# Taking chunk 0 of a gated MLP's second half column-first over two token tiles, and one more bank skipped before the spatial products

## The chip, the cores and the metric

The kernel runs on one core of a Trainium2 chip. The metric is the device time of one execution in microseconds (us). Three runs of the kernel as it stood gave 703.43, 703.61 and 705.5, median 703.61. One further execution was profiled: it took 703.75 us, and its profile covers a span of 702.0 us. Times inside the kernel are given in us from the start of that span.

## The reference

One transformer block on 2048 tokens of width 1024, in bfloat16, with two residual parts:

```python
h  = x + A(layernorm(x))      # qkv, attention over 8 earlier tokens at distance 0,2,..,14, then @ wo
h2 = h + B(layernorm(h))
# B:
z  = gelu(x @ w_in)                       # (2048, 3584)
z1 = z[..., :1792]
z2 = layernorm(z[..., 1792:])
g  = w_sp @ z2 + b_sp[:, None]            # (2048, 2048) times (2048, 1792)
return (z1 * g) @ w_out
```

The part that matters here is `z2`: the last 1792 columns of `x @ w_in`, through GELU, then normalised along those 1792 columns, so that a token's mean and variance need all 1792 of them. The product with `w_sp` (the spatial products) needs `z2` of all tokens.

## The kernel before

The tokens are cut into 4 chunks of 512 (`NCH`), a chunk into 4 token tiles of 128 (`TPC`, index `il`). The work of a chunk c is: layer norm and transposition; `qkv(c, ..)` (line 461); `attention(c)`, almost all of it on the vector engine (DVE): products of q with shifted k (line 525), sums of them by halving (lines 529, 532, 535), a small sum over heads on the tensor engine (PE, line 555), softmax, a small spreading matmul (line 617), products with v (lines 638, 641, 649); `head(c)`: the product with `wo` (line 716, 4 tiles of 16 matmuls), the residual on DVE (line 722), its squares on the scalar engine (ACT, line 727), the second layer norm (lines 678 to 687 and 759) and a transposition by DMA into `hnT`; `b_z2(c)` (line 790) and `b_z1(c)` (line 856). After all chunks come the spatial products in a form with seven products of halves instead of eight (`times`, line 1066), and the output product (line 1164).

`b_z2(c)` works token tile by token tile. A tile has 1792 columns, in two parts given by `win_specs`: `hf` 0 has 1024 columns and the weights `win0`, `hf` 1 has 768 columns and the weights `win1`. A part is summed over eight steps of 128 rows (`kt`), each step two matmuls (512 and 512 columns, or 512 and 256), 16 matmuls in all. Below, z2(il, hf) is one such part. Its GELU on ACT (line 797) frees the PSUM space, and when both parts of a tile are there, ACT sums the squares (line 805). When the four tiles of chunk 0 are done, DVE forms the variance (line 811 and lines 678 to 681), GpSimd (POOL) raises it to the power -1/2 (lines 685 and 687), and ACT normalises (line 831).

The order of work on PE, ACT, DVE and POOL is worked out before the program is written: `Order` holds a list of operations with an assumed duration, dependencies, priority and slots, plays them through in assumed time, and emits each engine's instructions in the order of the assumed starts. On the chip every engine then works through its own list in that order, and waits at an instruction whose inputs are not there. Operations of `b_z2` and `b_z1` have priority 6 and a running number and so fill the time in which PE has nothing of `attention` or `head` to do; `head` has priority 4 and up, the attention's matmuls 1.

Three accumulators (`new_acc`, `ps_acc`, each two banks of PSUM) are shared by all of this; two more banks belong to the attention. After `o_.run()` all eight banks go to the pool `psq`, from which the spatial products take single banks; before the first of them, `bank` tiles are asked for and never written, six of them in the kernel before.

The transfers that the change and the prediction touch: the weights `win0` to `win3` come on POOL's queue (`load_win`, line 387), one after the other; `win1` is issued after the load of k for attention 2. On the queue of SyncE (SP) stand, in this order around the change, the stores of the last qkv parts (line 473), three loads of `xr` (the residual's x tiles, three buffers, line 697), then the first store of h (line 724), the load of the fourth `xr` tile into the buffer of the first, and the other stores of h. The fourth load waits until ACT has squared the first tile (line 727), because that writes into the same buffer.

Before the change the engines have, in the stretch in question:

- PE: the last qkv part, z2(0,0) with 16 matmuls, 12 matmuls of z2(0,1), the 64 of `head(1)`, the remaining 4 of z2(0,1), then z2(1,0), z2(1,1) and so on to z2(3,1), then z1 of chunk 0, with the attention's matmuls of line 555 after 40 of them.
- DVE: the end of attention 1, two products of attention 2, the residual of `head(1)`'s first tile, two sums, the residual of the second tile, and so on.
- ACT: GELU of z2(0,0), squares of three tiles of `head(1)`, GELU of z2(0,1), squares of the fourth tile, then the rest.

Of the kernel before, what the change touches and what calls it, by code (L numbers as in the profile page):

```python
# [10 lines left out]
FP32 = mybir.dt.float32  # L11
BF16 = mybir.dt.bfloat16
# [3 lines left out]
ACTF = mybir.ActivationFunctionType  # L16
# [5 lines left out]
F, FH = 3584, 1792  # L22
P = 128
NT = S // P
CH = 512
NCH = S // CH
TPC = CH // P
TPP = 2 * TPC
KT = D // P
# [39 lines left out]
class Order:  # L69
# [6 lines left out]
    def add(self, eng, us, fn, deps=(), prio=5.0, lat=0.1, take=None, free=None, table=None):  # L76
        o = _Op()
        o.eng, o.us, o.fn, o.prio, o.lat, o.free, o.table = eng, us, fn, prio, lat, free, table
        o.take = (take,) if isinstance(take, str) else take or ()
        o.deps = [d if isinstance(d, tuple) else (d, d.lat) for d in deps if d is not None]  # L80
        o.start, o.end, o.n = None, None, len(self.ops)
        self.ops.append(o)
        return o
# [49 lines left out]
def kernel(  # L133
# [13 lines left out]
    V, A, T = nc.vector, nc.scalar, nc.tensor  # L147
# [42 lines left out]
    bp = bph_stack.enter_context(tc.tile_pool(name="bph", bufs=2))  # L190
# [4 lines left out]
    def new_acc():  # L195
        return ps_acc.tile([P, 2, CH], FP32, name="acc", tag="acc")
# [7 lines left out]
    l1 = bph_stack.enter_context(tc.tile_pool(name="ln1", bufs=2))  # L204
# [167 lines left out]
    for half in range(2):  # L372
        acc = new_acc()
# [8 lines left out]
    win_specs = [(FH, 1024), (FH + 1024, 768), (0, 1024), (1024, 768)]  # L382
    wins = {}
# [11 lines left out]
    add = o_.add  # L395
    G = {}

    def dma_op(us, fn, deps, lat=0.1, free=None):
        return add("DMA", us, fn, deps, lat=lat, free=free)
# [46 lines left out]
    def order():  # L446
        seq[0] += 1
        return 6.0 + seq[0] * 1e-3
# [225 lines left out]
    def batch_rstd(key, sums, sqs, n, pfx, deps, prio, cols=TPC):  # L674
        def moments():
            t = {k: bp.tile([P, cols], FP32, name=pfx + k, tag=pfx + k) for k in ("nmean", "msq", "var", "rstd", "nb")}
            G[key] = t
            V.tensor_scalar(t["nmean"][:], sums(), -1.0 / n, None, op0=ALU.mult)
            V.tensor_tensor(t["msq"][:], t["nmean"][:], t["nmean"][:], op=ALU.mult)
            V.scalar_tensor_tensor(t["var"][:], sqs(), 1.0 / n, t["msq"][:], op0=ALU.mult, op1=ALU.subtract)  # L680
            V.tensor_scalar(t["var"][:], t["var"][:], 0.0, EPS, op0=ALU.max, op1=ALU.add)
        s1 = add("DVE", 0.74, moments, deps, prio=prio)
        def root():
            t = G[key]
            nc.gpsimd.tensor_tensor(t["rstd"][:], t["var"][:], nhalf[:, 0:cols], op=ALU.pow)
            if cols == TPC:
                nc.gpsimd.tensor_tensor(t["nb"][:], t["nmean"][:], t["rstd"][:], op=ALU.mult)
        return add("POOL", 1.05 if cols < TPC else 1.6, root, [s1], lat=0.4 if cols < TPC else 1.2)
# [79 lines left out]
    hnTs, pools = {}, {}  # L768


    def b_z2(c):
        st = {}
        sqd = []
        for il in range(TPC):
            evs = []
            for hf in range(2):
                wd = win_specs[hf][1]
                deps = [G.get(("hnT", c, il), G["hnT", c]), G["win", hf]]
                for part in range(4):
                    def mm(part=part, hf=hf, il=il, wd=wd):  # L780
                        if part == 0:
                            st["acc"] = G["accz", c, il, hf] = new_acc()
                            if il == 0 and hf == 0:
                                st["sums"] = bp.tile([P, TPC, 2], FP32, name="sums", tag="sums")
                                st["sqs"] = bp.tile([P, TPC], FP32, name="sqs", tag="sqs")
                        accf = G["accz", c, il, hf][:].rearrange("p a b -> p (a b)")
                        for kt in range(2 * part, 2 * part + 2):
                            for n0 in range(0, wd, CH):
                                n1 = min(n0 + CH, wd)
                                T.matmul(accf[:, n0:n1], hnTs[c][:, il, kt, :], wins[hf][:, kt, n0:n1],  # L790
                                         start=(kt == 0), stop=(kt == KT - 1))
                    m_ = add("PE", 0.8634 if hf == 0 else 0.650, mm, deps, prio=order(), take="acc" if part == 0 else None)
                    deps = [(m_, 0.0)]
                def ev(hf=hf, il=il, wd=wd):
                    if hf == 0:
                        st["u", il] = l1.tile([P, FH], BF16, name="u", tag="x4k", bufs=4)
                    A.activation(st["u", il][:, hf * 1024:hf * 1024 + wd], G["accz", c, il, hf][:].rearrange("p a b -> p (a b)")[:, 0:wd],
                                 ACTF.Gelu_apprx_tanh, accum_out=st["sums"][:, il, hf:hf + 1])
                evs.append(add("ACT", 1.02 if hf == 0 else 0.93, ev, [m_] + ([G["z2st", c - 1, il]] if c else []),
                               prio=2.0, free="acc", lat=0.25, table="gelu"))  # L800
            if c == 0:
                evs[0].deps += [(o, 0.1) for o in wabs_ops]
            def sq(il=il):
                junk = pools["bq"].tile([P, FH], BF16, name="junk", tag="junk", bufs=1)[:]
                A.activation(junk, st["u", il][:], ACTF.Square, accum_out=st["sqs"][:, il:il + 1])
            sqd.append(add("ACT", 1.72, sq, evs + [G["open"]], prio=5.0, lat=0.25))
        each = c == NCH - 1
        def st_tot(il=0, n=TPC):
            if il == 0:
                st["stot"] = bp.tile([P, TPC], FP32, name="stot", tag="stot")  # L810
            V.tensor_tensor(st["stot"][:, il:il + n], st["sums"][:, il:il + n, 0], st["sums"][:, il:il + n, 1], op=ALU.add)
        if not each:
            s0 = add("DVE", 0.16, st_tot, sqd, prio=2.0)
            rs = batch_rstd(("l3", c), lambda: st["stot"][:], lambda: st["sqs"][:], FH, "l3", [s0], 2.0)
        for il in range(TPC):
            i = c * TPC + il
            if each:
                s0 = add("DVE", 0.16, lambda il=il: st_tot(il, 1), [sqd[il]], prio=0.5)
                rs = batch_rstd(("l3", c, il), lambda il=il: st["stot"][:, il:il + 1], lambda il=il: st["sqs"][:, il:il + 1],
                                FH, f"l2_{il}", [s0], 0.5, cols=1)  # L820
            def nrm(il=il, i=i, part=1):
                if each:
                    t = G["l3", c, il]
                    V.tensor_scalar(st["u", il][:], st["u", il][:], t["nmean"][:], t["rstd"][:], op0=ALU.add, op1=ALU.mult)
                    dma_w(z2_d[i * P:(i + 1) * P, :], st["u", il][:])
                    return
                t = G["l3", c]
                z2 = st["u", il]
                if Z2ACT[c] > il:
                    cols = slice(part * FH // 2, (part + 1) * FH // 2)  # L830
                    A.activation(z2[:, cols], st["u", il][:, cols], ACTF.Identity, scale=t["rstd"][:, il:il + 1], bias=t["nb"][:, il:il + 1])
                else:
                    V.tensor_scalar(z2[:], st["u", il][:], t["nmean"][:, il:il + 1], t["rstd"][:, il:il + 1], op0=ALU.add, op1=ALU.mult)
                if part:
                    dma(z2_d[i * P:(i + 1) * P, :], z2[:])
            if Z2ACT[c] > il:
                n_ = add("ACT", 1.05, lambda f=nrm: f(part=0), [rs], prio=5.5)
                n_ = add("ACT", 1.05, nrm, [n_], prio=5.5)
            else:
                n_ = add("DVE", 0.75 if each else 0.62, nrm, [rs], prio=0.6 if each else 2.5)  # L840
            G["z2st", c, il] = dma_op(3.0, lambda: None, [n_])
            G["z2n", c, il] = n_
# [208 lines left out]
    p2 = ctx.enter_context(tc.tile_pool(name="p2", bufs=2))  # L1051
    psq = ctx.enter_context(tc.tile_pool(name="psq", bufs=8, space=PSUM))

    for _ in range(6):
        psq.tile([P, CH], FP32, name="bank", tag="bank", bufs=8)

    def bank():
        return psq.tile([P, CH], FP32, name="bank", tag="bank", bufs=8)
# [9 lines left out]
    def f32(name):  # L1068
        return p2.tile([P, CH], FP32, name=name, tag=name)
# [12 lines left out]
    for pr in range(NCH // 2):  # L1082
# [5 lines left out]
        for i in range(NQ):  # L1088
# [3 lines left out]
            p1, p7, p5, u = f32("p1"), f32("p7"), f32("p5"), f32("u2")  # L1092
# [60 lines left out]
        for il in range(2 * TPC):  # L1153
# [15 lines left out]
            if t < NT - 1:  # L1169
                acc = [bank(), bank()]  # L1170
# [6 lines left out]
            else:  # L1177
                for n, (lo, hi) in enumerate(LAST_COLS):
                    acc = bank()
# [53 lines left out]
```

## Time and profile before

| what | value |
|---|---|
| median of three runs | 703.61 us |
| profiled execution, its own time / its span | 703.75 / 702.0 us |
| granted PE clock in the profile | 1.00 in every stage |
| PE busy | 693.4 us, 99% of the span |
| DVE busy | 508.4 us, 72% |
| ACT busy | 276.5 us, 39% |
| POOL busy | 120.7 us, 17% |
| z2 and z1 matmuls (lines 790 and 856) | 98.2 and 98.0 us |
| spatial products (line 1066) | 448 + 336 matmuls, on PE from 432.62 |
| load of `win1` on POOL's queue | issued 185.54, 11.8 us to landing |
| fourth `xr` load on SP's queue | issued 205.44, 8.0 us to landing |

Busy time of an engine alone says little here, since DVE is the busier engine's partner in some stages and idle in others. What is to be read is which engine waits for which at a given place. In the groups and the timeline a line gives the start, the length, the engine, the source line, and in brackets the idle time of that engine just before and what ended it. In the chain a line gives start, length, and what the time was spent on; matmul ends are modelled, so starts there stand some 0.17 us later than in the timeline.

### The profile page before, as it was taken

Reading aid. Unit: us, or ns where it says so; the run is one execution under the profiler, and the core shown is the slowest. Engines: PE = TensorE matmul, PEld = TensorE weight load, DVE = VectorE, ACT = ScalarE, POOL = GpSimd, SP = SyncE. Lnnn points to the kernel's source line nnn. Section 1 sums busy time; section 2 is a strip of 40 time slices with the busy share of each in tenths; the row PEclk is TensorE's granted clock in tenths of the full one; section 3 lists DMA queues with packets and bytes.
Section 4 is the critical chain, followed back from the end, with each engine's and each line's share of the span. In section 5 each row is a group of like instructions: output and inputs, shape, how many; then the busy total and the mean of one; then the engine's idle time right before and its main releaser. Section 6 shows DMA issues by size and latency. Waiting matters only on the chain.

```text
span 702.0 us, 8824 instructions
## 1 busy us (share of the span) xinstructions
PE 693.4 (99%) x3427; PEld 359.1 (51%) x3427; DVE 508.4 (72%) x614; ACT 276.5 (39%) x388; POOL 120.7 (17%) x113
## 2 busy tenths in 40 slices
PE   8999999999989999999999999999999999999998
PEld 7766665566635445444444544444444444444444
DVE  6899899999979899997994286556457845564222
ACT  4547652444227786755773643346100012111000
POOL 0100010011011111100201130534430023535000
PEclk9999999999999999999999999999999999999999
DMA  9968597577993669461774995699996125361121
GB/s 327 325 233 235 171 221 247 150 229 219 265 353 114 152 205 267 146 186 48 170 228 113 240 277 165 199 272 242 314 287 172 59 83 157 93 171 67 45 91 46
DMA packets 145193, 133.04 MB, mean 190 GB/s; under 512 B 68672, under 2 KB 117216, under 8 KB 145024
## 3 DMA queue, kind: packets, MB, share of 16 engines
q1 hardware_dynamic: 132688, 88.93, 44.6%
q0 software_dynamic: 7808, 32.97, 16.6%
q10 hardware_dynamic: 4656, 10.59, 4.7%
q8 instruction: 27, 0.44, 0.3%
q14 instruction: 14, 0.11, 0.0%
HBM read 75.24 MB, written 33.10 MB: 154 GB/s over the span
## 4 chain that ended last, share of the span: by engine, by line
PE 71%; DMA 2%; ACT 0%; DVE 0%; issue 0%
PE bank L1066 24%; PE acc L856 14%; PE bank L1164 14%; PE acc L790 13%; PE acc L716 6%; DMA win<-in_B_w_in_dram 2%; PE L L555 0%; ACT z1s L862 0%; PE pb L617 0%; DVE hr L1167 0%; PE rpq L1126 0%; PE rps L907 0%; PE pba L617 0%
## 5 line engine op out<-in xcount | busy, mean ns | idle before, releaser
L790 PE MATMUL acc<-win,hnT 128*128 128x512 bf16 (+1 forms) x512 | 98.2, 352 | 2.6 <-DMA win<-in_B_w_in_dram 2.6
L856 PE MATMUL acc<-hnT,win 128*128 128x512 bf16 x448 | 98.0, 379 | 0.0
L790 PEld LDWEIGHTS <-hnT 128*128 128x128 bf16 x512 | 49.9, 98 | 50.4 <-DMA win<-in_B_w_in_dram 3.1
L525 DVE TENSOR_TENSOR prod<-qT,kT 128x4096 bf16<-128x4096 bf16 x32 | 72.8, 2284 | 1.3 <-ACT kT L467 1.3
L1164 PEld LDWEIGHTS <-zg 128*128 128x128 bf16 x462 | 44.7, 98 | 52.4
L1066 PEld LDWEIGHTS <-zs 128*128 128x128 f16 x448 | 43.8, 98 | 52.9
L856 PEld LDWEIGHTS <-win 128*128 128x128 bf16 x448 | 43.7, 98 | 52.6 <-issue 0.7
L472 ACT CAST stg<-acc 128x1024 bf16<-128x1024 f32 x36 | 36.4, 1012 | 61.4 <-PE acc L461 54.7
L1102 ACT COPY p<-bank 128x512 f32<-128x512 f32 x14 | 8.2, 586 | 132.0 <-PE bank L1066 121.6
L1167 DVE SCALAR_TENSOR_TENSOR hr<-bank,rinv_w,hr 128x512 bf16<-128x512 f32 (+2 forms) x33 | 22.9, 731 | 51.4 <-PE bank L1164 51.2
L1164 PE MATMUL bank<-wout_a,zg 128*128 128x512 bf16 (+2 forms) x264 | 58.2, 373 | 0.0
L461 PE MATMUL acc<-xnT,wk 128*128 128x512 bf16 x256 | 56.5, 379 | 0.0
L461 PE MATMUL acc<-xnT,wv 128*128 128x512 bf16 x256 | 56.2, 379 | 0.0
L716 PE MATMUL acc<-wo_sb,av_oT 128*128 128x512 bf16 x256 | 56.1, 379 | 0.0
L1066 PE MATMUL bank<-rawa,z2f 128*128 128x512 f16 x224 | 52.9, 379 | 1.1 <-ACT z1s L862 1.1
L1066 PEld LDWEIGHTS <-z2f 128*128 128x128 bf16 x336 | 32.8, 98 | 40.8 <-issue 1.4
L1066 PE MATMUL bank<-rawb,zs 128*128 128x512 f16 x224 | 52.9, 379 | 0.0
L1066 PE MATMUL bank<-form,zs 128*128 128x512 f16 x224 | 50.6, 379 | 0.0
L461 PEld LDWEIGHTS <-wk 128*128 128x128 bf16 x256 | 36.5, 143 | 19.0 <-issue 0.8
L461 PEld LDWEIGHTS <-wv 128*128 128x128 bf16 x256 | 36.5, 144 | 18.7 <-issue 0.5
L1164 PE MATMUL bank<-wout_b,zg 128*128 128x512 bf16 (+2 forms) x198 | 44.4, 373 | 0.0
L862 ACT ACTIVATE z1s<-acc 128x1024 bf16<-128x1024 f32 x28 | 28.6, 1023 | 37.7 <-PE acc L856 33.4
(189 smaller groups left out, 944.2 us busy)
## 6 DMA issues: line engine op xcount, KB each, us to landing
z2f<-z_d SPq DMA_DIRECT2D x28, 512.0 KB, 5.4
qkv_d<-stg SPq DMA_DIRECT2D x36, 256.0 KB, 5.5
wn<-in_B_w_sp_dram ACTq DMA_DIRECT2D x16, 512.0 KB, 4.3
z1c<-z_d SPq DMA_DIRECT2D x14, 512.0 KB, 3.9
z_d<-z1s SPq DMA_DIRECT2D x21, 256.0 KB, 2.2
z_d<-u SPq DMA_DIRECT2D x12, 448.0 KB, 2.6
av_y<-av_z POOLq DMA_DIRECT2D x4, 1024.0 KB, 9.7
av_oT<-av_zz POOLq DMA_DIRECT2D x4, 1024.0 KB, 15.3
```

Source lines behind the costliest of these rows:

```text
L461: T.matmul(G[key][:, j, :].rearrange("p (a b) -> p a b", a=TPC), wv[:, kt, dl, :], xnT[c][:, :, kt, :], start=(kt == 0), stop=(kt == KT - 1))
L472: A.copy(stg[:], G[key][:])
L525: V.tensor_tensor(st["prod"][:], qT[:], kT[:, :, o:o + CH], op=ALU.mult)
L716: T.matmul(st["acc", il][:, nh, :], oTs[c][:, dl, il * P:(il + 1) * P], wo_sb[:, dl, nh * CH:(nh + 1) * CH], start=(dl == 0), stop=(dl == ...
L790: T.matmul(accf[:, n0:n1], hnTs[c][:, il, kt, :], wins[hf][:, kt, n0:n1], start=(kt == 0), stop=(kt == KT - 1))
L856: T.matmul(G["accy", c, fp][:, j, :].rearrange("p (a b) -> p a b", a=TPC), wt[:, kt, f0 * P:(f0 + 1) * P], hnTs[c][:, :, kt, :], start=(kt ...
L862: A.activation(z1s[:], G["accy", c, fp][:], ACTF.Gelu_apprx_tanh)
L1066: T.matmul(dst[:], wts[:, k, :], mov[:, k, :], start=(first and k == 0), stop=(k == HK - 1), skip_group_check=not first)
L1102: A.copy(p1[:], k1[:])
L1164: T.matmul(outs, zg[:, f, il * P:(il + 1) * P], wt[:, f0, lo:hi], start=(f == 0), stop=(f == NF - 1))
L1167: V.scalar_tensor_tensor(hr[:, lo:hi], acc[:, 0:hi - lo], rv[:, t:t + 1], hr[:, lo:hi], op0=ALU.mult, op1=ALU.add)
```

## The change

In chunk 0 alone, the second and third turn of `b_z2` change places: z2(0,0), z2(1,0), z2(0,1), z2(1,1), and then tiles 2 and 3 as before. The loops over `il` and `hf` become one loop over a list of turns, with the list of GELUs kept per tile; the squares of a tile are added when its second part is. For the other chunks the turns are as they were. Since the work is put in order by `Order`, what moves on the engines follows from its assumed times. Apart from that, seven instead of six `bank` tiles are asked for and left unwritten before the spatial products.

```diff
@@ -771,33 +771,38 @@
     def b_z2(c):
         st = {}
         sqd = []
-        for il in range(TPC):
-            evs = []
-            for hf in range(2):
-                wd = win_specs[hf][1]
-                deps = [G.get(("hnT", c, il), G["hnT", c]), G["win", hf]]
+        turns = [(il, hf) for il in range(TPC) for hf in range(2)]
+        if c == 0:
+            turns[1:3] = (1, 0), (0, 1)
+        evs_ = [[] for _ in range(TPC)]
+        for il, hf in turns:
+            evs = evs_[il]
+            wd = win_specs[hf][1]
+            deps = [G.get(("hnT", c, il), G["hnT", c]), G["win", hf]]
...
+            evs.append(add("ACT", 1.02 if hf == 0 else 0.93, ev, [m_] + ([G["z2st", c - 1, il]] if c else []),
+                           prio=2.0, free="acc", lat=0.25, table="gelu"))
+            if hf == 0:
+                continue
             if c == 0:
                 evs[0].deps += [(o, 0.1) for o in wabs_ops]
...
@@ -1051,7 +1056,7 @@
     p2 = ctx.enter_context(tc.tile_pool(name="p2", bufs=2))
     psq = ctx.enter_context(tc.tile_pool(name="psq", bufs=8, space=PSUM))
 
-    for _ in range(6):
+    for _ in range(7):
         psq.tile([P, CH], FP32, name="bank", tag="bank", bufs=8)
```

More of the change, by code (lines that the diff above doesn't have):

```diff
@@ L773, in b_z2 @@
         sqd = []
-        for il in range(TPC):
-            evs = []
-            for hf in range(2):
-                wd = win_specs[hf][1]
-                deps = [G.get(("hnT", c, il), G["hnT", c]), G["win", hf]]
[L779 to L800, printed above, removed]
@@ new lines, in b_z2, with mm, ev @@
+        turns = [(il, hf) for il in range(TPC) for hf in range(2)]
[6 more added lines that the diff above has]
+            deps = [G.get(("hnT", c, il), G["hnT", c]), G["win", hf]]
+            for part in range(4):
+                def mm(part=part, hf=hf, il=il, wd=wd):
+                    if part == 0:
+                        st["acc"] = G["accz", c, il, hf] = new_acc()
+                        if il == 0 and hf == 0:
+                            st["sums"] = bp.tile([P, TPC, 2], FP32, name="sums", tag="sums")
+                            st["sqs"] = bp.tile([P, TPC], FP32, name="sqs", tag="sqs")
+                    accf = G["accz", c, il, hf][:].rearrange("p a b -> p (a b)")
+                    for kt in range(2 * part, 2 * part + 2):
+                        for n0 in range(0, wd, CH):
+                            n1 = min(n0 + CH, wd)
+                            T.matmul(accf[:, n0:n1], hnTs[c][:, il, kt, :], wins[hf][:, kt, n0:n1],
+                                     start=(kt == 0), stop=(kt == KT - 1))
+                m_ = add("PE", 0.8634 if hf == 0 else 0.650, mm, deps, prio=order(), take="acc" if part == 0 else None)
+                deps = [(m_, 0.0)]
+            def ev(hf=hf, il=il, wd=wd):
+                if hf == 0:
+                    st["u", il] = l1.tile([P, FH], BF16, name="u", tag="x4k", bufs=4)
+                A.activation(st["u", il][:, hf * 1024:hf * 1024 + wd], G["accz", c, il, hf][:].rearrange("p a b -> p (a b)")[:, 0:wd],
+                             ACTF.Gelu_apprx_tanh, accum_out=st["sums"][:, il, hf:hf + 1])
+            evs.append(add("ACT", 1.02 if hf == 0 else 0.93, ev, [m_] + ([G["z2st", c - 1, il]] if c else []),
+                           prio=2.0, free="acc", lat=0.25, table="gelu"))
+            if hf == 0:
+                continue
```

## The prediction

> **What bounds the kernel now.** I read the page's busy rows first, then the chain of waits that ended last, then the waits, then the timelines of PE and DVE from 190 to 245 us.
>
> ```profile
> span 702.0 us, 8824 instructions
> PE 693.4 (99%) x3427; PEld 359.1 (51%) x3427; DVE 508.4 (72%) x614; ACT 276.5 (39%) x388; POOL 120.7 (17%) x113
> ```
>
> PE works nearly all the time, so a microsecond leaves the span only if PE has less to do or idles less. The chain, in order of time:
>
> ```profile
> 185.54 11.79 DMA win<-in_B_w_in_dram
> 197.33 0.05 issue
> 197.38 2.12 PE acc L790 x12
> 199.50 13.81 PE acc L716 x64
> ...
> 240.76 0.55 PE L L555 x8
> ...
> 368.19 0.86 PE acc L716 x4
> ...
> 431.53 0.02 issue
> 431.55 1.03 ACT z1s L862
> 432.58 0.04 issue
> 432.62 72.68 PE bank L1066 x336
> ```
>
> From 197.38 on the chain is PE work, except for 1.1 us at 431.5. Ahead of it stands the load of `win1`, landed at 197.33. PE's timeline (start, length, idle time before) shows the wait:
>
> ```profile
> 191.15 3.62 PE L790 MATMUL acc<-win,hnT 128*128 128x512 bf16 x16
> 197.38 2.12 PE L790 MATMUL acc<-win,hnT 128*128 128x512 bf16 x12 [2.62 <-DMA win<-in_B_w_in_dram]
> ```
>
> The second line is z2(0,1), the first work to need `win1`. DVE's timeline shows who shares the stretch:
>
> ```profile
> 195.29 4.49 DVE L525 TENSOR_TENSOR prod<-qT,kT 128x4096 bf16<-128x4096 bf16 x2
> 203.00 1.23 DVE L722 SCALAR_TENSOR_TENSOR hb<-acc,xr 128x1024 bf16<-128x1024 f32 x1 [3.21 <-PE acc L716]
> ...
> 209.90 1.22 DVE L722 SCALAR_TENSOR_TENSOR hb<-acc,xr 128x1024 bf16<-128x1024 f32 x1 [0.68 <-PE acc L716]
> ...
> 239.76 0.43 DVE L535 TENSOR_TENSOR part<-prod 128x512 bf16<-128x512 bf16 x1
> 241.36 1.23 DVE L564 TENSOR_REDUCE mx<-L 128x128 f32<-128x1024 f32 x1 [1.17 <-PE L L555]
> ```
>
> The last sum of attention 2 ends at 240.19; PE reaches line 555, which reads it, at 240.76. That is 0.57 us of slack: if PE comes 2.8 us earlier and DVE does not, PE waits there instead.
>
> **The wait itself.** Matmuls of 512 columns start every 0.2158 us (13.81 us for 64). The 16 of z2(0,0) therefore leave PE free at 191.15 + 3.45 = 194.60; work resumes at 197.38. At issue pace the hole is 2.78 us. In the instruction order of the changed kernel PE does z2(0,0), 8 matmuls of z2(1,0), the 64 of `head(1)`, the other 8 of z2(1,0), then z2(0,1) and z2(1,1). Number and shapes of matmuls are the same, so the change of PE work is 0.
>
> The new order runs: z2(1,0) from 194.60, `head(1)` from 196.33 (before: 199.34 on the timeline, so 3.0 earlier), until 210.14; z2(1,0) ends at 211.87; z2(0,1) starts there, 14.5 us after `win1` landed; z1 starts about 229.2 (before 231.96); line 555 is reached at 237.98.
>
> **What must be ready earlier.** The `head(1)` matmuls need the attention's output: the DVE operation before 195.29 ends at 195.38, 0.95 us ahead. Accumulators: z2(1,0) now holds one of three through `head(1)`, as z2(0,1) did. The last qkv part is copied out by 193.41 and the GELU of z2(0,0) is over at 195.8, both ahead of the head tiles that reuse them (196.33, 199.78); the third and fourth head tile reuse what line 722 freed at about 201.2 and 204.6, needed at 203.23 and 206.69. Cost 0, with 2 us of cover.
>
> DVE, replayed by its own rows in the new order: two products until 199.78; the first residual at 200.00, when its matmuls end (idle 0.22, was 3.21); one sum until 202.30; the second residual at 203.45 (idle 1.15); four sums until 207.4; the third, whose matmuls ended at 206.85, until 208.5; a sum and a product until 211.10; the fourth. Idle time falls from 3.21 + 0.68 to 0.22 + 1.15, a gain of 2.52. The last sum of attention 2 then ends at 237.67, 0.31 us ahead of PE at 237.98. So line 555 costs 0, with thin cover.
>
> **Moved transfers.** Line 727's first squares, and with them the fourth `xr` load, come 3.0 earlier: issue at 202.43 instead of 205.44. The transfers issued from 204 to 207.2 show its price, and that no hardware-queue packet moved while `win2` and `win3` were streaming:
>
> ```profile
> q0 software_dynamic: 288, 1.19, 102.3%
> issues: line engine op xcount, KB each, median us to landing
> h_d<-hb SPq DMA_DIRECT2D x1, 256.0 KB, 7.1
> xr<-in_A_x_dram SPq DMA_DIRECT2D x1, 256.0 KB, 8.0
> ```
>
> At 8.0 us it lands at 210.4, ahead of the fourth residual (211.10). The bounds are 2.2 us (the median of the stores of `z1s` in the issue rows, landing at 204.6) and 17.7 us (the slowest `xr` load of this stretch, landing at 220.1). I take 8.0, the same load in the same company. POOL's loads (`win2`, `win3`, v) hang on `win1`'s landing and do not move. SP's queue keeps its order here; later one z2 store stands one z1 store earlier, in a stretch with 2 us of room.
>
> [...]
>
> **Moved ACT work.** The GELU of z2(1,0) (1.11 us with its accumulator, at 212.1) now stands ahead of the squares of the head's fourth tile (213.2 to 214.3), which DVE asks for at 215.6. Replayed on, ACT ends the fourth tile's squares (line 805) at 232.6 (before 234.97); DVE asks for them at 233.45. ACT then has three normalising halves, not two, ahead of the third z1 GELU: they end at 240.35 against PE's 240.25, cost 0.1 beside PE. The exponentials come at 242.7 (before 245.51), so the whole attention chain moves with PE. From there on the order of every engine is the old one, and attention 3 has 368.19 - 366.52 = 1.67 us of slack besides. Cost 0.
>
> **The seventh bank tile.** In the built program of both kernels the first spatial product lies in bank 0 and the last z1 accumulator in banks 0 and 1; all later banks agree too. The tile asked for and never written moves nothing. So the 1.1 us before 432.62, a wait for the last z1 GELU, stays. Gain 0.
>
> **Sum.** 2.78 us from the hole, nothing given back: 703.75 - 2.78 = 700.97 for the profiled execution. That one lay 0.14 above the median, 703.61 - 2.78 = 700.83. I say 700.9, rounding to the side where the slack of 0.31 is thin.
>
> **Rivals.**
>
> 1. *POOL and ACT late.* POOL's `l2nb` took 1.29 us at 218.26, beside a DVE product (217.21 to 219.49), and 0.22 at 137.22, with DVE in just the order that the change now gives. If it falls behind the product after all, normalising starts at 221.5 instead of 218.4, line 805 ends at 235.2, DVE waits 1.7, and PE 1.4 at line 555: 702.3. [...]
>
> 2. *The fourth `xr` load lands no earlier than before,* at 213.4, since packets of that queue began only about 208 in the trace. The fourth residual comes at 213.46, DVE loses 2.36, and PE waits 2.36 - 0.31 = 2.05 at line 555. Gain 0.7: 702.9. Against it: the 4 us delay is counted from the issue in the trace, and the queue ahead of it is the same.
>
> 3. *Slower, by the same load.* If it takes 16.5 us, the median of this stretch's four, it lands at 218.9. Line 555 follows the landing by 26.6 us (the DVE work from the fourth residual, 211.10, to the last sum, 237.67): 245.5, 4.7 behind the old 240.76, so 708.3. It turns into a loss from a landing after 214.2, and into a loss over 0.3% after 216.3. Against it: the loads that took 15.6 to 17.7 stood behind four qkv stores and `win1`; now only one 256 KB store of h is ahead.
>
> 4. *The bank tile does work after all* and the first product starts on landing of PE: another 1.07, so 699.8. The built order speaks against it.
>
> **Chances.** Forecast (700.4 to 701.4) 0.67; rival 1 or another small wait at line 555, 701.4 to 702.5, 0.12; rival 2, 0.12; rival 3, 0.06; rival 4, 0.03. Range 700.4 to 703.0: it leaves out rivals 3 and 4 and little else. A difference under 0.3%, 2.1 us here, is about what cannot be told from no change; faster by more means below 701.5. That holds the forecast, rival 4 and a third of rival 1: 0.74. Within 0.3%: 0.20. Slower: 0.06.
>
> **What would show it.** Right: no idle of PE for `win1` near 194.6; `head(1)` from about 196.3; the fourth `xr` load landed by 211; line 555 at about 238 without idle ahead of it; 1.1 us of idle still before the first spatial product; the span about 699.2. Wrong: idle of PE at line 555 of attention 2, with DVE waiting at the fourth line 722 (rivals 2, 3) or at line 811's sum (the changed file's line 816) for line 805 (rival 1); or a first spatial product that does not wait for ACT.

## The result, and the profile after

The changed kernel took 701.23 us (median of 6 runs, 701.01 to 701.34), the kernel before 703.75 us (6 runs, 703.43 to 705.5). The ratio is 0.9958, interval 0.9945 to 0.9971: faster by 0.42%, above the 0.3% that a measurement of this kernel can tell. The forecast was 700.9 us with a range of 700.4 to 703.0. The profiled execution of the changed kernel took 701.22 us.

One thing has to be told to read the times of the kernel before: they fall into two groups. Over all measurements below it ran 64 times, 31 times between 702.88 and 703.89 (median 703.51) and 33 times between 705.05 and 706.15 (median 705.26), never between the two. The changed kernel has one group. Where the upper one comes from is one of the findings.

The page of the changed kernel, span and busy rows (PEld is PE's loading of weights):

```profile
span 699.4 us, 8823 instructions
PE 693.8 (99%) x3427; PEld 359.4 (51%) x3427; DVE 508.1 (73%) x614; ACT 276.6 (40%) x388; POOL 117.6 (17%) x113
```

PE does the same 3427 matmuls in the same busy time within 0.4 us, in a span shorter by 2.6. So it idles less. The chain of work that ended last (start, length, what), through the stretch that was changed and at its later narrow places:

```profile
191.50 5.18 PE acc L793 x24
196.68 13.81 PE acc L716 x64
210.49 19.03 PE acc L793 x104
229.53 8.63 PE acc L861 x40
238.16 0.55 PE L L555 x8
...
365.60 0.86 PE acc L716 x4
...
428.95 1.03 ACT z1s L867
430.03 72.68 PE bank L1071 x336
```

The load of `win1` is gone from the chain: matmuls follow each other from 191.50 to 238.71. Line 555 of attention 2 comes at 238.16 where it came at 240.76. The piece of ACT ahead of the first spatial product (line 1071, in the kernel before 1066) is still there. PE's timeline, with no idle time in brackets:

```profile
191.34 5.34 PE L793 MATMUL acc<-win,hnT 128*128 128x512 bf16 x24
196.52 13.98 PE L716 MATMUL acc<-wo_sb,av_oT 128*128 128x512 bf16 x64
210.33 19.20 PE L793 MATMUL acc<-win,hnT 128*128 128x512 bf16 x104
```

The 24 of line 793 are z2(0,0) and the first half of z2(1,0); then `head(1)`, without a wait. DVE's timeline (bracket: idle time before, and what ended it):

```profile
200.17 1.23 DVE L722 SCALAR_TENSOR_TENSOR hb<-acc,xr 128x1024 bf16<-128x1024 f32 x1 [0.20 <-PE acc L716]
...
203.62 1.23 DVE L722 SCALAR_TENSOR_TENSOR hb<-acc,xr 128x1024 bf16<-128x1024 f32 x1 [1.08 <-PE acc L716]
...
211.20 1.23 DVE L722 SCALAR_TENSOR_TENSOR hb<-acc,xr 128x1024 bf16<-128x1024 f32 x1
...
237.26 0.43 DVE L535 TENSOR_TENSOR part<-prod 128x512 bf16<-128x512 bf16 x1
238.76 1.23 DVE L564 TENSOR_REDUCE mx<-L 128x128 f32<-128x1024 f32 x1 [1.07 <-PE L L555]
```

DVE gained as much as PE: two short waits of 0.20 and 1.08 us instead of the old 3.21 and 0.68, and the last sum of attention 2 is done at 237.69, 0.47 us ahead of line 555. The fourth residual, at 211.20, waits for nothing, but only just. The transfers issued from 201.4 to 205.0 (name, engine, count, size each, time to landing):

```profile
q0 software_dynamic: 348, 1.43, 101.8%
issues: line engine op xcount, KB each, median us to landing
h_d<-hb SPq DMA_DIRECT2D x2, 256.0 KB, 7.7
xr<-in_A_x_dram SPq DMA_DIRECT2D x1, 256.0 KB, 8.5
```

The fourth `xr` load, issued at 202.62, landed 8.5 us later at 211.11, 0.09 us before DVE wanted it. As in the kernel before, only the queue of the weight loads moved packets in this stretch. The first packet of SP's queue moved at 205.08, 3.65 us after the issue of the first h store (201.43). From then on both queues moved, with nearly the same number of packets (queue, packets, MB, share; from 206 to 211):

```profile
q0 software_dynamic: 325, 1.42, 71.6%
q1 hardware_dynamic: 323, 0.60, 32.1%
```

### The profile page after: what moved, and what is told of

It is laid out like the page before. It is cut to its first block, busy times and chain, and to the rows that moved or that the text cites. A ratio compares the mean times of both kernels' runs of the same rounds, so it can differ in the third digit from the quotient of the medians.

```text
span 699.4 us, 8823 instructions
## 1 busy us (share of the span) xinstructions
PE 693.8 (99%) x3427; PEld 359.4 (51%) x3427; DVE 508.1 (73%) x614; ACT 276.6 (40%) x388; POOL 117.6 (17%) x113
## 4 chain that ended last, share of the span: by engine, by line
PE 99%; ACT 0%; DVE 0%; issue 0%
PE bank L1071 24%; PE acc L461 22%; PE acc L793 14%; PE acc L861 14%; PE bank L1169 14%; PE acc L716 8%; PE acc L303 2%; PE wps L226 1%; PE L L555 0%; PE tpt L299 0%; PE pb L617 0%; ACT z1s L867 0%; ACT xnT L300 0%; DVE hr L1172 0%; PE tpa L299 0%
```

## The experiments

My theory after the result: the whole gain is PE's idle time in front of z2(0,1); the order of the turns is only the means; and the seventh bank tile does nothing. Rivals: part of the gain comes from the bank; part comes from the new order as such, through DVE or ACT; or more was to be had with another order. Two questions came up on the way: what the wait ahead of the first spatial product belongs to, and why the kernel before has two groups of run times.

### The turns alone, and the banks alone

The first is the changed kernel with six bank tiles left unwritten, the second the kernel before with seven.

```diff
-    for _ in range(7):
+    for _ in range(6):
```

> The changed kernel with six unwritten bank tiles again, so only the turns of z2 in chunk 0 differ from the kernel before. Theory: the whole gain is the hole for win1, so 701.2, as the changed kernel, with 1.1 us of idle before the first spatial product. Rival: the seventh tile has a share, then between 701.2 and 703.7.

Measured: 701.19 us (5 runs, 700.97 to 701.48), ratio 0.996 (0.9947 to 0.9972). The first spatial product starts at 430.00, again after 1.11 us of idle time.

```diff
-    for _ in range(6):
+    for _ in range(7):
```

> The kernel before with seven unwritten bank tiles, turns as before. Theory: nothing moves, 703.7 with the hole of 2.6 us and the 1.1 us before the first spatial product. Rival: the first product's wait shrinks or goes, then down to 702.6.

Measured: 703.73 us (12 runs, 703.18 to 705.6), ratio 0.9996 (0.9984 to 1.0007). Its lower group has a median of 703.48, that of the kernel before 703.51. So the turns carry the whole gain, and the seventh tile none.

This run brought something else. Its 12 runs split as those of the kernel before do, 9 from 703.18 to 703.95 and 3 at 705.3 to 705.6, and the profiled execution was of the upper group, 705.3 us. Its stretches (stretch, length, busy time of PE, PEld, DVE, ACT, POOL with counts, granted PE clock, DMA share, GB/s):

```profile
194.90:197.40 2.50, 0.02 (x1) 0.00 (x0) 2.50 (x2) 1.11 (x2) 0.00 (x0) 0.94 1.03 385
197.40:201.00 3.60, 3.59 (x13) 1.79 (x14) 2.53 (x2) 0.00 (x0) 2.63 (x3) 0.57 0.74 215
201.00:205.00 4.00, 4.00 (x21) 1.78 (x19) 0.46 (x1) 0.00 (x0) 0.00 (x0) 1.00 1.03 404
```

The same stretch of the kernel before, whose profiled execution was of the lower group:

```profile
197.40:201.00 3.60, 3.60 (x20) 1.95 (x21) 2.39 (x2) 0.00 (x0) 2.63 (x3) 1.00 0.67 200
```

After the idle time the granted clock of the upper group is 0.57 on the mean of 3.6 us, and 13 matmuls run where 20 did. The trace's own record of the clock has 0.5 from 197.10 to 200.51, which is 3.41 us. The groups of this stretch by shape (line, operation, count, busy time, mean ns of one, idle before), of this kernel:

```profile
L790 PE MATMUL acc<-win,hnT 128*128 128x512 bf16 x6 | 3.5, 588 | 2.5 <-DMA win<-in_B_w_in_dram 2.5
L790 PE MATMUL acc<-win,hnT 128*128 128x256 bf16 x6 | 2.3, 384 | 0.0
```

and of the kernel before:

```profile
L790 PE MATMUL acc<-win,hnT 128*128 128x512 bf16 x6 | 2.0, 381 | 2.6 <-DMA win<-in_B_w_in_dram 2.6
L790 PE MATMUL acc<-win,hnT 128*128 128x256 bf16 x6 | 1.6, 272 | 0.0
```

The 12 matmuls of z2(0,1) take 3.63 us on the timeline instead of 2.12: 1.51 of the 1.75 us by which the groups differ. The mean granted clock of each run says the same of all of them. A stretch of 3.41 us at 0.5 in a span of 703.5 makes a mean of 0.998, and 0.997 fits if the span's last 0.7 us are at 0.5 as well, as they are in the profile before. Of the 58 runs of the kernel before that stood beside the experiments, the 31 of the upper group have 0.997 or 0.998, the 27 of the lower group 0.999 or 1.000; of this kernel's 12, the 3 upper ones have 0.997 or 0.998 and the others 0.999 or 1.000. So the upper group is the halved clock. That it is the hole which halves it, and so has a second price beside its time, is what the last three experiments test.

### The old order without the wait

The kernel before, with z2(0,1) reading `win0`, which is long there.

```diff
-                                T.matmul(accf[:, n0:n1], hnTs[c][:, il, kt, :], wins[hf][:, kt, n0:n1],
+                                wsrc = wins[0] if (c, il, hf) == (0, 0, 1) else wins[hf]
+                                T.matmul(accf[:, n0:n1], hnTs[c][:, il, kt, :], wsrc[:, kt, n0:n1],
```

> The kernel before, its order untouched, but z2(0,1) multiplies by the columns of win0 instead of win1 (this part of z2 is computed with the wrong weights), so PE has no load to wait for there. Theory: the gain is the hole and not the order, so no idle near 194.6, about 701.2, and in no run the half clock that the profile of the kernel with seven bank tiles showed behind the hole (3.4 us at 0.5 from 197.1), so no runs 1.7 us above the others. Rival: the new order of DVE and ACT has a share of its own, then above 701.6.

Measured: 701.08 us (6 runs, 700.8 to 702.22), ratio 0.9953 (0.9939 to 0.9968), span 699.4. Line 555 at 238.09. With the old order and no hole the time is that of the changed kernel, so the order as such is worth nothing that these runs can tell, and the gain is the hole. DVE's timeline shows how near the next wait is:

```profile
211.67 1.23 DVE L722 SCALAR_TENSOR_TENSOR hb<-acc,xr 128x1024 bf16<-128x1024 f32 x1 [0.59 <-DMA xr<-in_A_x_dram]
...
238.77 1.23 DVE L564 TENSOR_REDUCE mx<-L 128x128 f32<-128x1024 f32 x1 [0.50 <-PE L L555]
```

Here the fourth `xr` load landed at 211.57, DVE waited 0.59 us for it, and the slack at line 555 took that up.

### The fourth `xr` load later

The changed kernel; in chunk 1 the load hangs on the squares of the second tile, not of the first.

```diff
-                if il + XRB < TPC:
+                if c == 1:
+                    if il == 1:
+                        xr_load(XRB)
+                elif il + XRB < TPC:
                     xr_load(il + XRB)
```

> The changed kernel with the fourth xr load of head(1) issued after the squares of the second tile instead of the first, some 3.5 us later (issue about 206, landing about 213 to 214.5 instead of 211.1). Theory of rivals 2 and 3 of the prediction: DVE waits at the fourth residual until the landing, the last sum of attention 2 comes later by the same, and PE waits at line 555 less the slack that the profile after shows there (238.16 - 237.69 = 0.47); for a landing at 214.5 DVE loses 3.3, PE 2.8, so 704.0; for 213, 702.5. Rival: the wait of DVE is taken up elsewhere and the time stays within 0.5 of 701.2.

Measured: 703.16 us (10 runs, 702.84 to 704.21), 1.93 above the changed kernel; ratio 0.998 (0.9969 to 0.9991). The load was issued at 205.00 and landed at 213.38, which is where rival 2 put it. DVE's timeline:

```profile
213.47 1.22 DVE L722 SCALAR_TENSOR_TENSOR hb<-acc,xr 128x1024 bf16<-128x1024 f32 x1 [2.57 <-DMA xr<-in_A_x_dram]
```

PE's timeline:

```profile
214.75 14.87 PE L796 MATMUL acc<-win,hnT 128*128 128x512 bf16 x80 [0.25 <-DVE hb L722]
...
238.18 0.40 PE L555 MATMUL L<-part,csb 128*32 128x512 bf16 x4
240.00 0.40 PE L555 MATMUL L<-part,csb 128*32 128x512 bf16 x4 [1.42 <-DVE part L535]
```

The 2.57 us of DVE turn into 0.25 and 1.42 us of PE, the latter in the middle of line 555, whose second half reads the last sum. The span is 701.1, 1.7 above the changed kernel's. Rival 2's mechanism was right and its price nearly (702.9; the 0.25 us ahead of line 796 were not in it); the change escaped it by 0.09 us on DVE and 0.47 at line 555.

### Four tiles column-first

The changed kernel; in chunk 0 all four tiles first take their first columns.

```diff
-            turns[1:3] = (1, 0), (0, 1)
+            turns = [(il, hf) for hf in range(2) for il in range(TPC)]
```

> The changed kernel with all four tiles of chunk 0 taking their first 1024 columns and then all four the rest. Theory: the hole is closed by 8 matmuls ahead of head(1) already, so more of the same gains nothing: 701.2, unless the squares, which now come late and together on ACT, are late for DVE's sum (rival 1 of the prediction), then up to 702.6 with PE idle at line 555. Rival: each tile turned round gains, then below 700.8.

Measured: 701.23 us (5 runs, 700.88 to 701.36), ratio 0.9951 (0.9935 to 0.9968), no idle time of PE in the stretch. Nothing more was to be had: two tiles already reach across the wait.

### Whose wait it is ahead of the first spatial product

The prediction put the 1.1 us down to bank 0, which the first product shares with the last z1 accumulator. The changed kernel with one more tile taken and written, so that, in the built program, the first product lies in bank 7, which belonged to the attention:

```diff
+    pre = bank()
+    V.memset(pre[:, 0:1], 0.0)
     bB = wt_["rows"]
```

> The changed kernel with one further bank tile of which DVE clears one column before the spatial products; that tile takes bank 0 and the first product then lies in bank 7, which the attention left long before. Theory of the prediction (the wait is that of bank 0, shared with the last z1 accumulator): the 1.1 us before the first product go, 700.1. Rival: the wait belongs to the pool, which was opened over the closed accumulators as a whole, whatever the bank; then 1.1 us stay and the time is 701.2. The built order speaks for the rival, since the first product still waits for the last GELU there.

Measured: 701.07 us (6 runs, 700.84 to 701.65), ratio 0.9958 (0.9945 to 0.9971). PE's timeline has the same wait:

```profile
429.89 1.89 PE L1073 MATMUL bank<-rawa,z2f 128*128 128x512 f16 x8 [1.11 <-ACT z1s L867]
```

So it is not the bank. The next kernel takes the space for the products from two pools, one of which (two banks) is opened as soon as the attention's is closed and before that of the accumulators is; the first products come from it.

```diff
     bph_stack.close()
+    psh = ctx.enter_context(tc.tile_pool(name="psh", bufs=2, space=PSUM, side="right"))
     ps_stack.close()
...
-    psq = ctx.enter_context(tc.tile_pool(name="psq", bufs=8, space=PSUM))
+    psq = ctx.enter_context(tc.tile_pool(name="psq", bufs=6, space=PSUM))
+    taken = [0]
...
+    def bank(shape=(P, CH), dt=FP32, name="bank"):
+        pool, n = (psh, 2) if taken[0] % 8 < 2 else (psq, 6)
+        taken[0] += 1
+        return pool.tile(list(shape), dt, name=name, tag="bank", bufs=n)
```

> The changed kernel with the eight banks in two pools: two banks that lay outside the accumulators, opened before the accumulators are closed, and six after; the first and second product of a round lie in the two. Both theories: the first product no longer waits for the last z1 GELU, 1.1 us less, 700.1. If something else (the sums of z2 on DVE, a load) stood close behind that wait, the gain is smaller and an idle time of PE shows up at the second, third or fourth product.

Measured: 699.87 us (5 runs, 699.75 to 700.07), ratio 0.9941 (0.9928 to 0.9953), span 697.8. PE's timeline, with no idle time before the product:

```profile
428.48 1.89 PE L1072 MATMUL bank<-rawa,z2f 128*128 128x512 f16 x8
```

The wait belongs to the pool, as this program is built: the first product, in a tile of a pool that was opened over the whole of PSUM, waits for the last reader of what lay there, in bank 0 and in bank 7 alike (1.11 us each); from the two pools it does not wait. This version beats both kernels, by 1.36 us the changed one. The bracket has 1.11 us from the modelled end of the last matmul; at issue pace PE paused 430.03 - (404.58 + 112 x 0.2158) = 1.28 us, as the hole was 2.78 us for a bracket of 2.62.

### The clock after the hole

Three kernels that start from the kernel before and change only the hole. In the first, the first 6 of the 16 matmuls of z2(0,1) read `win0`, so that PE has work for about 1 us more before it needs `win1`.

```diff
+                                wsrc = wins[0] if (c, il, hf) == (0, 0, 1) and kt < 3 else wins[hf]
```

> The kernel before, its order untouched, but the first three of eight steps of z2(0,1) multiply by win0 (six matmuls with the wrong weights), so PE works 0.97 us on before it waits for win1: a hole of some 1.6 us by the profile's count instead of 2.6. [...]

Measured: 702.53 us (11 runs, 702.22 to 703.01, one group), ratio 0.9973 (0.9963 to 0.9983). PE's timeline:

```profile
197.65 1.14 PE L791 MATMUL acc<-win,hnT 128*128 128x512 bf16 x6 [1.75 <-DMA win<-in_B_w_in_dram]
```

The lower group's 703.51, less the 0.87 us by which the hole is shorter (2.62 less 1.75), gives 702.64. No run lies near the upper group, and the mean granted clock is 1.000 in all 11.

The second keeps the wait but fills it with 11 matmuls whose sums the next one overwrites.

```diff
+                        if (c, il, hf, part) == (0, 0, 1, 0):
+                            for _ in range(11):
+                                T.matmul(accf[:, 0:CH], hnTs[c][:, il, 0, :], wins[0][:, 0, 0:CH], start=True, stop=True)
```

> The kernel before with 11 extra matmuls of 512 columns between z2(0,0) and z2(0,1), into the accumulator that z2(0,1) then overwrites: 2.37 us of PE work that counts for nothing, inside the hole of 2.78 us; the wait for win1 stays. Theory: what puts the kernel before 1.7 us up in about half of its runs is the half clock after the idle of PE, so with PE kept working every run lies near the lower group, 703.5, and none above 704.5. Rival: it is the wait, or the load itself, that comes late in those runs; then the two groups stay, 703.5 and 705.3.

Measured: 703.62 us (12 runs, 703.35 to 704.26, one group), ratio 0.999 (0.9981 to 0.9999). The kernel before, beside it, ran 17 times: 9 at 702.97 to 703.78, 8 at 705.08 to 705.65. PE's timeline:

```profile
194.65 2.54 PE L789 MATMUL acc<-win,hnT 128*128 128x512 bf16 x11
197.03 2.12 PE L793 MATMUL acc<-win,hnT 128*128 128x512 bf16 x12
```

In this execution `win1` was there by 197.03 and left no wait behind the filling. The time stays that of the lower group and the upper group is gone: the useless work costs 0.1 to 0.2 us (703.62 against that group's 703.51 over all runs and 703.39 beside this kernel), and keeps the clock up (mean 1.000 in all 12).

The third makes the hole longer: a part of `win1` is loaded twice.

```diff
+        if k == 1:
+            dma_w(t[:, 0:1, :], win_view[:, 0:1, c0:c0 + wd])
         i_ = dma_w(t[:], win_view[:, :, c0:c0 + wd])
```

> The kernel before with one eighth of win1 loaded ahead of win1 into the same place, so that the load of win1 starts when that has landed, some 2 to 5 us later, and the hole grows by as much, to 5 to 8 us. [...]

Measured: 710.34 us (4 runs, 709.92 to 711.07), ratio 1.0087 (1.0071 to 1.0103). PE's timeline:

```profile
202.26 4.00 PE L792 MATMUL acc<-win,hnT 128*128 128x512 bf16 x12 [7.57 <-DMA win<-in_B_w_in_dram]
```

Its stretches, with columns as above (the granted clock is the third number from the end):

```profile
198.00:202.00 4.00, 0.00 (x0) 0.00 (x0) 1.72 (x1) 0.00 (x0) 0.00 (x0) 0.71 0.56 216
202.00:206.00 4.00, 3.74 (x12) 1.79 (x13) 0.00 (x0) 0.00 (x0) 2.63 (x3) 0.50 0.41 108
206.00:210.00 4.00, 4.00 (x20) 1.78 (x18) 0.07 (x1) 0.00 (x0) 0.00 (x0) 0.94 1.02 402
```

The record of the clock has 0.5 from 199.67 to 206.49, 6.82 us, twice the 3.41 us of the kernel with seven bank tiles. PE resumed at 202.26 and ran 4.2 us at half clock, which loses 2.1. The lower group's 703.5, plus 4.95 of longer hole (7.57 less 2.62), plus 2.1 gives 710.5; measured 710.34. All four runs have a mean granted clock of 0.993 to 0.995, where 6.82 us at 0.5 make 0.995 and 3.41 us more make 0.993: after a hole of this length (7.57 us in the profile) every run paid.

## Why the prediction was right, and where it was off

- **The wait itself** (2.78 us, nothing given back): right. The wait is gone, and the experiment that took it away in the old order gained the same. On the profiled executions the span fell by 2.6, since z2(0,0) began 0.19 us later in this one (191.34 instead of 191.15), and 2.78 less 0.19 is 2.59.
- **What must be ready earlier** (cost 0): right. `head(1)` at 196.52 for a predicted 196.33, the first two residuals at 200.17 and 203.62 for 200.00 and 203.45, the fourth at 211.20 for 211.10, the last sum at 237.69 for 237.67. All but the last are the 0.1 to 0.2 us of the later start. The slack at line 555 was 0.47, not 0.31.
- **Moved transfers** (8.0 us, landing 210.4): right in its effect, off in size. The load took 8.5 us and landed at 211.11. Its cover was 0.09 us, not the 0.7 of the working; the delayed load shows what that cover was worth, 1.9 us. The prediction's reading that no packet of a hardware queue moved while `win2` and `win3` were streaming was wrong: it rests on the window from 204 to 207.2, and from 208.0 on the kernel before moved packets of both queues (291 and 293 from 209 to 213.4). So the load's 8 us are a delay of the queue and then a shared pace. The delay, from the issue of the first h store to the first packet, was 3.60 to 3.75 us in four profiles; what causes it no run shows. In the first 3.6 us after the issue of the first h store the page of the window has one queue only; behind them both moved, 325 and 323 packets from 206 to 211.
- **Moved ACT work** (cost 0): right. The squares of the fourth tile (line 805, in the changed file 810) ended at 232.51 for 232.6. DVE's sum of line 816 came at 233.54 for 233.45, but it reads the GELU's sums; the squares are read by line 680, at 234.19, so the cover was larger than the working had it; the three normalising halves ended at 240.56, with PE not waiting.
- **The seventh bank tile** (gain 0): the number was right and the reason wrong. The bank that the first product gets does not matter, bank 7 having the same wait as bank 0, since the wait is the pool's. So the bank tile could not bring the fourth rival's 699.8; two pools give what it promised, 699.87.
- **The first rival** (POOL late): did not happen, line 687 took 0.22 us at 218.09. **The second** was right in mechanism and price and missed its condition by very little. **The third** needed a landing after 214.2.
- **The size of the sum** (700.9, measured 701.23): the profiled execution was forecast at 700.97 and took 701.22, of which 0.19 is the later start at z2(0,0). For the median I subtracted the hole of one execution, 2.78 by issue pace. That hole varies with the landing of `win1`: PE's bracket was 2.62 in the profile before, 2.49 in that of the kernel with seven banks, and in the kernel with the filled hole `win1` had landed before 197.03, some 0.3 earlier. From the lower group's 703.51 to 701.23 are 2.28 us. That the typical hole is shorter than the profiled one is argued from these three executions, not shown.
- **The term that was left out**: the halved clock. The profile before was of the lower group and had clock 1.00 everywhere, so no row of it showed the term. Against the upper group the change gains 705.26 - 701.23 = 4.0 us, and these were about half of its runs. The three runs given at the start had it in sight: one of them, 705.5, lay 1.9 above the others, and I took it for scatter.

## What to carry to other kernels

The idle stretch of TensorE in front of one late load (2.62 us) was filled by ready work that reached to the next ready stage; 8 matmuls of the next tile were enough, and more tiles brought nothing (701.23 us with two tiles and with four). Before believing such a gain, replay the engine that runs nearly level with TensorE and time every load that moves with it: 0.47 us and 0.09 us were all that kept this gain whole. And list the single run times: the two groups with nothing between them meant a price of 1.75 us that one profile did not show, and the wait at the change of PSUM pools, 1.11 us, lay in the pools' opening and closing, not in the banks.

## What the runs showed of the hardware

With an idle stretch of TensorE of 2.49 us, up to 197.41, the granted clock was 0.5 from 197.10 to 200.51 (profile of the kernel with seven bank tiles); with one of 2.62 us, in the profile before, it stayed at 1.00. By the upper group of times, or by the mean granted clock, it was halved in 33 of 64 runs of the kernel before (2.62 us idle in its profile) and in 3 of 12 of the one with seven banks (2.49 us); with 1.75 us in none of 11; with 1.42 us (the late load) in none of 10; with the same wait filled by useless matmuls in none of 12; in none of 33 runs of the kernels without the hole (mean clock 0.999 or 1.000 in all); with 7.57 us in all four (0.993 to 0.995).

The stretch at 0.5 is 3.41 us long in the record with the wait of 2.49 us, and 6.82 us in that with 7.57 us. In the profile of the short hole the clock stayed at 1.00, in the 3.4 us that hold all its 1.75 us of idle time and in those behind them:

```profile
194.25:197.65 3.40, 1.65 (x11) 0.79 (x9) 3.40 (x2) 1.82 (x3) 0.00 (x0) 1.00 1.05 395
197.66:201.07 3.41, 3.41 (x18) 1.72 (x18) 2.28 (x2) 0.00 (x0) 2.63 (x3) 1.00 0.62 176
```

and in that with the halved clock, where PE was busy for 1.23 us of the 3.41 us ahead of 197.10:

```profile
193.69:197.10 3.41, 1.23 (x6) 0.38 (x4) 3.41 (x2) 1.34 (x3) 0.00 (x0) 1.00 1.03 394
197.11:200.51 3.40, 3.10 (x10) 1.48 (x11) 2.82 (x2) 0.00 (x0) 2.59 (x3) 0.50 0.75 213
```

The length of the wait alone does not settle it, as the profiles with 2.49 and 2.62 us show. What decides in which runs of one kernel the clock is halved, no run shows; no profile here has a wait for `win1` between 1.75 and 2.49 us, or between 2.62 and 7.57 us.
